# Attention scores in four row tiles, with q and k turned by VectorE

## The chip, the cores and the metric

One core of one Trainium2 chip. Times are device microseconds of that core, medians over several executions; "span" is the length of one profiled execution. The experiments ran as several jobs, on different chips, so each ratio is to the kernel before in the same job. TensorE, VectorE, ScalarE and GpSimd are called PE, DVE, ACT and POOL in the profile; PEld is the weight load of TensorE.

## The reference

Sliding-window attention with ALiBi (8 batches, 8 heads, 576 rows, head size 64, window 128), then a two-layer network with ELU on the 4608 resulting rows (512 to 2048 to 512):

```python
scores = scale * np.matmul(q, k.transpose(0, 1, 3, 2))
mask = (rel >= 0) & (rel < window)                       # rel = query position - key position
scores = np.where(mask, scores - slopes * np.abs(rel), -1e9)
attn = softmax(scores)
x = (attn @ v) ...reshape(B * S, H * D)
h = x @ w_in
out = np.where(h > 0, h, np.exp(np.minimum(h, 0)) - 1) @ w_out
```

One weakness of the comparison: the drawn q and k are small (0.1 times normal), so the scores hardly differ from the ALiBi term. "Right" below means right by construction.

## The kernel before

The kernel works in slots, emitted in order on every engine. A slot holds one piece of the hidden layer (`hp`, 8 or 16 matmuls), one quarter of an output block (`op`, 4 matmuls), and some attention work. In the kernel before, TensorE turns q and k with transposes into PSUM, and ScalarE and VectorE copy them out. ALiBi and mask enter as extra rows of the score matmul:

```python
def transposes(b, hp):                       # two heads a call
    t = ps_s.tile([128, 2, 2, 4, 2, 32], F16, name="tp", tag="sps")
    for g in range(2):
        for w in (1, 0):
            for j in range(2):
                nc.tensor.transpose(t[:, g, w, :, j, :], stq[b][...], ident)
    ...                                      # two copies to QK, by ACT or DVE

def mm(o, h, kc, qc, n):                     # scores: all 128 rows of the array
    nc.tensor.matmul(t[:, o:o + n], qk[0:r, h, 1, kc:kc + 128], qk[0:r, h, 0, qc:qc + n], ...)
e = ex[b, s] = EX[count[0] % 4]
nc.scalar.activation(e[:, 0:512], t, AF.Exp, scale=0.125)
# then cut(): DVE takes the minimum with a band

def hidden(t, j):
    ...                                      # hp <- xT, w_in
    nc.scalar.activation(e, p, AF.Exp)
    nc.gpsimd.tensor_scalar(out=e, in0=e, scalar1=1.0, scalar2=0.0, op0=ALU.min, op1=ALU.max)
def elu(t, j):                               # one slot later; frees one of the two hp banks
    V.scalar_tensor_tensor(out=gs[t][...], in0=e, scalar=1.0, in1=hp, op0=ALU.subtract, op1=ALU.max)
```

The q and k loads give partition p of each block of 128 rows the rows 4p to 4p+3, so the columns come out in another order, and masks, v and output rows are arranged to suit.

The softmax here doesn't subtract the row's maximum and nothing guards it: scores larger than these inputs give would overflow.

Of the kernel before, what the change touches and what calls it, by code (L numbers as in the profile page):

```python
# [10 lines left out]
I32 = mybir.dt.int32  # L11
# [4 lines left out]
BIG = 60000.0  # L16
# [3 lines left out]
def kernel(  # L20
# [13 lines left out]
    NP = H // 2  # L34
    NFC = FF // 128
    NTB = NTOK // 512
    MID = S // 2
    XBAR = 2
    RING = 3 * S
    VW = D + 2  # L40
    V = nc.vector
# [5 lines left out]
    ps_s = ctx.enter_context(tc.tile_pool(name="ps_s", bufs=2, space=PSUM))  # L47
    ps_v = ctx.enter_context(tc.tile_pool(name="ps_v", bufs=2, space=PSUM))
    ps_x = ctx.enter_context(tc.tile_pool(name="ps_x", bufs=1, space=PSUM))
# [7 lines left out]


    DM = one([128, 384], F16, "DM")
    cI = one([128, H, 128], F16, "cI")  # L60
    band = one([128, 384], F16, "band")




    QK = [one([128, H, 2, 640], F16, f"QK{i}") for i in range(2)]
    VP = [one([128, 5, H, VW], F16, f"VP{i}") for i in range(2)]
    EX = [one([128, 576], F16, f"EX{i}") for i in range(4)]
    w_in_sb = one([128, 4, FF], F16, "wi")
    w_out_sb = one([128, NFC, DO], F16, "wo")  # L70
    xT = one([128, 4, RING], F16, "xT")


    stq, stt, vf, vs = {}, {}, {}, {}

    def load_qk(b, w, h0=0, h1=H):

        if b not in stq:
            stq[b] = stage.tile([128, 2, H, 4, D], F16, name="stq")
        nc.gpsimd.dma_start(  # L80
            stq[b][:, w, h0:h1, :, :].rearrange("p h j d -> p h (j d)"),
            (q, k)[w][b, h0:h1, 0:512, :].rearrange("h (p j) d -> p h (j d)", j=4))

    def load_half(b, w, a):
        if b not in stq:
            stq[b] = stage.tile([128, 2, H, 4, D], F16, name="stq")
        nc.gpsimd.dma_start(
            stq[b][64 * a:64 * a + 64, w, :, :, :].rearrange("p h j d -> p h (j d)"),
            (q, k)[w][b, :, 256 * a:256 * a + 256, :].rearrange("h (p j) d -> p h (j d)", j=4))

    def load_v_half(b, a):
        if b not in vs:
            vs[b] = stage.tile([128, H, 4, D], F16, name="vs", tag="vs", bufs=2)
        nc.gpsimd.dma_start(
            vs[b][64 * a:64 * a + 64, :, :, :].rearrange("p h j d -> p h (j d)"),
            v[b, :, 256 * a:256 * a + 256, :].rearrange("h (p j) d -> p h (j d)", j=4))

    def load_tail(b, w):
        if b not in stt:
            stt[b] = stage.tile([64, 2, H, D], F16, name="stt")  # L100
        nc.gpsimd.dma_start(
            stt[b][:, w, :, :], (q, k)[w][b, :, 512:576, :].rearrange("h s d -> s h d"))

    def load_v4(b):

        vs[b] = stage.tile([128, H, 4, D], F16, name="vs", tag="vs", bufs=2)
        nc.gpsimd.dma_start(vs[b].rearrange("p h j d -> p h (j d)"),
                            v[b, :, 0:512, :].rearrange("h (p j) d -> p h (j d)", j=4))

    def load_v4_tail(b):  # L110
        nc.gpsimd.dma_start(VP[b % 2][0:64, 4, :, 0:D],
                            v[b, :, 512:576, :].rearrange("h s d -> s h d"))

    def place_v4(b, n):
        for j in range(4):
            V.tensor_copy(VP[b % 2][32 * j:32 * j + 32, n, :, 0:D],  # L116
                          vs[b][32 * n:32 * n + 32, :, j, :])

    def load_v(b, n):

        t = vf[b, n] = stage.tile([128, H, D], F32, name="vf", tag="vf", bufs=3)
        if b == 3 and n < 3:
            nc.gpsimd.memset(t[:, 0, 0:1], 0.0)
        if n < 4:
            for j in range(4):
                nc.sync.dma_start(
                    t[32 * j:32 * j + 32, :, :],
                    v[b, :, 128 * n + j:128 * n + 128:4, :].rearrange("h p d -> p h d"))
        else:
            nc.sync.dma_start(t[0:64, :, :], v[b, :, 512:576, :].rearrange("h p d -> p h d"))  # L130
# [11 lines left out]
    def load_wo(i, n):  # L142
        nc.gpsimd.dma_start(
            w_out_sb[:, 4 * i:4 * i + 4 * n, :],
            moe_w_out[512 * i:512 * i + 512 * n, :].rearrange("(c p) d -> p c d", p=128))
# [3 lines left out]
    with tc.manual_schedule():  # L149

        row = one([128, 1], I32, "row")
        col = one([128, 128], I32, "col")
        posi = one([128, 576], I32, "posi")
        nc.gpsimd.iota(row, pattern=[[0, 1]], base=0, channel_multiplier=1)
        nc.gpsimd.iota(col, pattern=[[1, 128]], base=0, channel_multiplier=0)
        load_half(0, 1, 0)
        load_half(0, 0, 0)
        nc.gpsimd.iota(posi[:, 0:512].rearrange("p (n j i) -> p n j i", j=4, i=32),
                       pattern=[[128, 4], [1, 4], [4, 32]], base=0, channel_multiplier=0)
        nc.gpsimd.iota(posi[:, 512:576], pattern=[[1, 64]], base=512, channel_multiplier=0)  # L160
        load_v_half(0, 0)
        load_wi(0)
        load_wi(1)
        load_half(0, 1, 1)
        load_half(0, 0, 1)
        load_v_half(0, 1)
        load_wi(2)
        load_wi(3)

        def small(name, dt=F32):  # L170
            return one([128, 1], dt, name)

        rowf = small("rowf")
        V.tensor_copy(rowf, row)
        V.tensor_scalar(out=ident, in0=col, scalar1=rowf, scalar2=None, op0=ALU.is_equal)
        for h in range(H):
            nc.scalar.mul(cI[:, h, :], ident, 8.0 * 2.0 ** (-8.0 * (h + 1) / H))

        kdiv, kmod, kpos = small("kdiv", I32), small("kmod", I32), small("kpos")
        V.tensor_scalar(out=kdiv, in0=row, scalar1=5, scalar2=None, op0=ALU.logical_shift_right)  # L180
        V.tensor_scalar(out=kmod, in0=row, scalar1=31, scalar2=None, op0=ALU.bitwise_and)
        V.scalar_tensor_tensor(out=kpos, in0=kmod, scalar=4.0, in1=kdiv, op0=ALU.mult, op1=ALU.add)
        for i in range(2):
            V.memset(VP[i][:, :, :, D:D + 1], 1.0)
        nd = one([128, 384], F32, "nd")
        nm = one([128, 384], F32, "nm")

        def seen(c, t, key, off, n):

            V.tensor_scalar(out=nd[:, c:c + n], in0=t, scalar1=key, scalar2=-1.0,  # L190
                            op0=ALU.subtract, op1=ALU.mult)
            if off:
                V.tensor_scalar(out=nd[:, c:c + n], in0=nd[:, c:c + n], scalar1=float(-off),
                                scalar2=None, op0=ALU.add)

        def unseen(c, n, bound, op):
            V.tensor_scalar(out=nm[:, c:c + n], in0=nd[:, c:c + n], scalar1=bound, scalar2=-BIG,
                            op0=op, op1=ALU.mult)

        def join(c, n):  # L200
            V.tensor_tensor(out=DM[:, c:c + n], in0=nd[:, c:c + n], in1=nm[:, c:c + n], op=ALU.add)

        seen(0, posi[:, 0:256], kpos, 0, 256)
        unseen(0, 128, 0.0, ALU.is_gt)
        unseen(128, 128, -127.0, ALU.is_lt)
        join(0, 256)

        def last_blocks():
            seen(256, posi[:, 512:576], kpos, -384, 64)
            seen(320, posi[:, 512:576], rowf, -512, 64)  # L210
            unseen(256, 64, -127.0, ALU.is_lt)
            unseen(320, 64, 0.0, ALU.is_gt)
            join(256, 128)

        def bands():
            V.tensor_scalar(out=band, in0=DM, scalar1=-1000.0, scalar2=BIG, op0=ALU.is_gt, op1=ALU.mult)

        def zeros():
            for i in range(2):
                V.memset(QK[i][0:64 + 64 * i, :, 1, 576:640], 0.0)  # L220
                V.memset(VP[i][64:128, 4, :, 0:D], 0.0)
            for e in EX:
                V.memset(e[:, 512:576], 0.0)


        g_, r_ = slice(64, 96), slice(96, 128)
        gof = small("gof")
        is96, is97, isx = small("is96"), small("is97"), small("isx")
        TQ = one([128, 576], F16, "TQ")
        TK = one([128, 640], F16, "TK")  # L230
        gi = one([128, 320], I32, "gi")
        pm = one([128, 576], F32, "pm")

        def groups():
            V.tensor_scalar(out=gof, in0=rowf, scalar1=-8.0, scalar2=1024.0, op0=ALU.mult, op1=ALU.add)
            V.tensor_scalar(out=gi[g_, 0:256], in0=posi[g_, 0:256], scalar1=gof[g_, :], scalar2=None,
                            op0=ALU.add)
            V.tensor_scalar(out=gi[g_, 256:320], in0=posi[g_, 512:576], scalar1=gof[g_, :],
                            scalar2=None, op0=ALU.add)
            V.tensor_scalar(out=gi[g_, :], in0=gi[g_, :], scalar1=255, scalar2=None,  # L240
                            op0=ALU.bitwise_and)

        def terms():

            V.tensor_scalar(out=is96, in0=rowf, scalar1=96.0, scalar2=None, op0=ALU.is_equal)
# [10 lines left out]
        def group_rows():  # L256
# [5 lines left out]
            for t in (TQ, TK):  # L262
                V.tensor_copy(t[g_, 256:512], t[g_, 0:256])
# [6 lines left out]
        def fill_k(i):  # L270
            nc.sync.dma_start(QK[i][r_, :, 1, :], QK[1 - i][r_, :, 1, :])

# [355 lines left out]
```

## Time and profile before

| | before |
|---|---|
| time, median | 366.84 us (366.28 to 369.29) |
| TensorE busy | 94% |
| VectorE busy | 67% |
| ScalarE / GpSimd busy | 57% / 40% |
| mean granted TensorE clock | 0.995 |

How to read it: TensorE is busy nearly throughout, and its work sets the end. The prediction shows the lines. One batch from the middle (busy us of each engine in the stretch, instruction counts in brackets, then clock and transfers):

```profile
195.78:232.55 36.77, 36.30 (x377) 26.70 (x377) 25.96 (x59) 23.58 (x40) 16.65 (x26) 1.00 0.67 111
```

In order: PE, PEld, DVE, ACT, POOL. TensorE has 36.3 of 36.8 us; VectorE has 11 us to spare.

### The profile page before, as it was taken

What the parts mean: (1) busy time and instruction counts of PE and PEld (TensorE: products, weight loads), DVE (VectorE), ACT (ScalarE), POOL (GpSimd) and SP (SyncE); (2) the same over time, 40 slices, a digit from 0 to 9 for tenths busy, and PEclk for the clock granted to TensorE, in tenths of its full rate; (3) what the DMA queues carried; (4) which work ended last, traced back from release to release, by engine and by line L of the source; (5) the groups of instructions that cost most, each with busy time, mean ns of one, the idle gap of its engine ahead of it and who ended that gap; (6) DMA issues with size and microseconds to landing.
All of it is one profiled execution on the core that took longest, in us unless ns stands there. A gap on an engine that the chain in (4) does not pass through costs nothing.

```text
span 363.7 us, 9613 instructions
## 1 busy us (share of the span) xinstructions
PE 340.3 (94%) x3790; PEld 251.6 (69%) x3790; DVE 243.5 (67%) x574; ACT 206.7 (57%) x349; POOL 145.7 (40%) x229
## 2 busy tenths in 40 slices
PE   6878997999979999989999999999999999999994
PEld 6766775777647667767777777777777777666651
DVE  6479889678886776666676767776776756634430
ACT  4355583666537655765566665666567565543431
POOL 9146623434314723472346334642433232233320
PEclk9899999999999999999999999999999999999999
DMA  8999999839243973497448934793631222211113
GB/s 114 198 206 119 228 107 183 151 80 155 38 103 89 133 108 84 110 128 110 98 94 127 127 88 100 120 136 82 102 84 45 52 47 45 51 43 47 29 43 73
DMA packets 81948, 37.06 MB, mean 102 GB/s; under 512 B 51952, under 2 KB 77296, under 8 KB 81904
## 3 DMA queue, kind: packets, MB, share of 16 engines
q0 software_dynamic: 34064, 15.40, 35.5%
q1 hardware_dynamic: 47840, 21.06, 25.6%
q8 instruction: 29, 0.48, 0.6%
q14 instruction: 15, 0.12, 0.1%
HBM read 36.70 MB, written 9.44 MB: 127 GB/s over the span
## 4 chain that ended last, share of the span: by engine, by line
PE 65%; DVE 14%; ACT 9%; DMA 7%; issue 3%; POOL 1%; SPq 0%; ACTq 0%; POOLq 0%
PE hp L451 27%; PE op L492 25%; PE sp L348 5%; ACT QK L322 5%; DVE VP L116 4%; DMA vs<-in_v_dram 3%; PE av L394 3%; DVE g L463 3%; ACT EX L372 2%; DVE QK L324 2%; ACT e L455 2%; DVE EX L380 2%; DMA xT<-xn 2%; DMA stq<-in_q_dram 1%; DVE xn L415 1%
## 5 line engine op out<-in xcount | busy, mean ns | idle before, releaser
L456 POOL TENSOR_SCALAR e<-e 128x512 f32<-128x512 f32 x144 | 88.6, 615 | 199.9 <-ACT e L455 199.9
L451 PE MATMUL hp<-xT,wi 128*128 128x256 f16 (+3 forms) x1536 | 150.3, 246 | 8.1 <-DVE g L463 3.6
L451 PEld LDWEIGHTS <-wi 128*128 128x128 f16 x1536 | 121.5, 98 | 49.9 <-DVE g L463 5.5
L455 ACT ACTIVATE e<-hp 128x512 f32<-128x512 f32 x144 | 86.0, 597 | 119.0 <-PE hp L451 110.0
L492 PE MATMUL op<-wo,g 128*128 128x512 f16 x576 | 146.4, 379 | 0.0
L463 DVE SCALAR_TENSOR_TENSOR g<-e,hp 128x512 f16<-128x512 f32 x144 | 98.0, 681 | 23.9 <-POOL e L456 22.7
L380 DVE TENSOR_TENSOR EX<-EX,band 128x512 f16<-128x512 f16 x112 | 49.8, 445 | 57.1 <-ACT EX L372 57.0
L372 ACT ACTIVATE EX<-sp 128x512 f16<-128x512 f32 x128 | 75.9, 593 | 13.3 <-PE sp L368 8.6
L492 PEld LDWEIGHTS <-g 128*128 128x128 f16 x576 | 51.2, 98 | 36.9
L348 PE MATMUL sp<-QK 128*128 128x128 f16 (+3 forms) x576 | 49.8, 213 | 0.0
L394 PE MATMUL av<-VP,EX 128*128 128x65 f16 x576 | 38.6, 193 | 4.3 <-DVE EX L380 2.7
L394 PEld LDWEIGHTS <-EX 128*128 128x128 f16 x576 | 31.6, 98 | 8.7 <-DVE EX L380 4.2
L415 DVE TENSOR_TENSOR xn<-av,rden 128x256 f16<-128x256 f32 x80 | 34.0, 424 | 2.8
L348 PEld LDWEIGHTS <-QK 128*128 128x128 f16 (+1 forms) x576 | 31.3, 97 | 1.0 <-issue 0.2
L496 ACT COPY ob<-op 128x512 f32<-128x512 f32 x36 | 21.1, 586 | 14.3 <-PE op L492 6.4
L322 ACT COPY QK<-tp 64x1024 f16<-64x1024 f16 x28 | 28.1, 1005 | 1.6 <-PE tp L312 1.4
L414 DVE RECIPROCAL rden<-av 128x4 f32<-128x4 f32 x80 | 14.4, 180 | 16.0 <-PE av L394 14.6
L134 POOL TENSOR_SCALAR VP<-vf 128x512 f16<-128x512 f32 (+1 forms) x25 | 19.5, 779 | 2.7 <-DMA vf<-in_v_dram 2.7
L324 DVE COPY QK<-tp 64x1024 f16<-64x1024 f16 x28 | 19.2, 684 | 1.1 <-PE tp L312 0.8
L312 PE MATMUL tp<-ident,stq 128*128 128x128 f16 x224 | 17.1, 219 | 2.3 <-ACT QK L322 1.0
L312 PEld LDWEIGHTS <-stq 128*128 128x128 f16 x224 | 13.8, 98 | 3.4 <-issue 3.2
L116 DVE COPY VP<-vs 32x512 f16<-32x512 f16 x48 | 14.9, 310 | 1.3 <-DMA vs<-in_v_dram 0.5
(70 smaller groups left out, 118.5 us busy)
## 6 DMA issues: line engine op xcount, KB each, us to landing
out_dram<-ob SPq DMA_DIRECT2D x128, 64.0 KB, 1.7
vf<-in_v_dram SPq DMA_DIRECT2D x80, 64.0 KB, 2.3
stq<-in_k_dram POOLq DMA_DIRECT2D x7, 512.0 KB, 6.4
stq<-in_q_dram POOLq DMA_DIRECT2D x7, 512.0 KB, 7.5
wi<-in_moe_w_in_dram POOLq DMA_DIRECT2D x4, 512.0 KB, 13.8
wo<-in_moe_w_out_dram POOLq DMA_DIRECT2D x4, 512.0 KB, 15.1
QK<-TQ SPq DMA_DIRECT2D x2, 576.0 KB, 8.0
vs<-in_v_dram POOLq DMA_DIRECT2D x2, 512.0 KB, 9.9
```

What stands on the lines that cost most here:

```text
L312: nc.tensor.transpose(t[:, g, w, :, j, :], stq[b][:, w, 2 * hp + g, 2 * j:2 * j + 2, :].rearrange("p a d -> p (a d)"), ident)
L322: nc.scalar.copy(o, i)
L348: nc.tensor.matmul(t[:, o:o + n], qk[0:r, h, 1, kc:kc + 128], qk[0:r, h, 0, qc:qc + n], start=b > 0 or o == 0, stop=b > 0)
L372: nc.scalar.activation(e[:, 0:512], t, AF.Exp, scale=0.125)
L380: V.tensor_tensor(out=e, in0=e, in1=band[:, c:c + n].unsqueeze(1).broadcast_to([128, 512 // n, n]), op=ALU.min)
L394: nc.tensor.matmul(a[:, l, :], e[:, c:c + 128], vp[:, n, h, 0:D + 1], start=st, stop=sp)
L415: V.tensor_tensor(out=xnt[b, i][:, 4 * half:4 * half + 4, :], in0=a[:, :, 0:D], in1=r.unsqueeze(2).broadcast_to([128, 4, D]), op=ALU.mult)
L451: nc.tensor.matmul(p[:, l * w + u0:l * w + u1], w_in_sb[:, c, fc * 128:(fc + 1) * 128], xT[:, c, x0:x0 + u1 - u0], start=(c == 0), stop=(c ...
L455: nc.scalar.activation(e, p, AF.Exp)
L456: nc.gpsimd.tensor_scalar(out=e, in0=e, scalar1=1.0, scalar2=0.0, op0=ALU.min, op1=ALU.max)
L463: V.scalar_tensor_tensor(out=gs[t][:, f0:f0 + nf, c0:c0 + w], in0=sh(es.pop((t, j))), scalar=1.0, in1=sh(hps.pop((t, j))), op0=ALU.subtrac ...
L492: nc.tensor.matmul(ops[t], gs[t][:, fc, ts * 128:(ts + 1) * 128], w_out_sb[:, fc, :], start=(fc == 0), stop=(fc == NFC - 1))
```

## The change

Its intent: run the scores with a contraction of 32 in four row tiles of TensorE, so that four heads go through the array at once; have VectorE turn q and k in squares of 32 (no TensorE transposes, no PSUM, no copies out); keep rows in natural order, so that one transfer loads large contiguous pieces and output rows go out in one; and put ALiBi and mask into a table that multiplies the exponentials. The core of the diff, cuts marked:

```diff
-    QK = [one([128, H, 2, 640], F16, f"QK{i}") for i in range(2)]
+    TAB = one([128, 2, 4, 512], F16, "TAB")
+    QT = [one([128, 2, 2, S], F16, f"QT{i}") for i in range(2)]
+    KT = [one([128, 2, 2, 640], F16, f"KT{i}") for i in range(2)]
+    sp = ps_s.tile([128, 4, 512], F32, name="sp", tag="sp")      # four banks, one set
...
+    def load_qk(b, w, g):                                        # R = 18
+        nc.gpsimd.dma_start(
+            st[b][32 * g:32 * g + 32, w, :, :, :].rearrange("p h r d -> p h (r d)"),
+            (q, k)[w][b, 2 * g:2 * g + 2, :, :].rearrange("h (i r) d -> i h (r d)", r=R))
+
+    def turn_qk(b, w, h2, dh):
+        o = (QT, KT)[w][b % 2][:, h2, dh, 0:S].rearrange("p (i r) -> p r i", r=R)
+        V.transpose(o, st[b][:, w, h2, :, 32 * dh:32 * dh + 32])
...
+    def scores(b, k_):
+        for o, kb, q0, n in parts:
+            for dh in range(2):
+                for g in range(4):
+                    r = slice(32 * g, 32 * g + 32)
+                    nc.tensor.matmul(sp[:, g, o:o + n], kt[r, h2, dh, ...], qt[r, h2, dh, ...],
+                                     start=dh == 0, stop=dh == 1, tile_position=(32 * g, 0))
...
+    def weigh(b, k_, gp):                                        # 1024 elements a call
+        V.tensor_tensor(out=e, in0=e, in1=t, op=ALU.mult)
...
+            order = [(w, h2, dh) for h2 in range(2) for w in (1, 0) for dh in range(2)]
+            for n, what in enumerate(order):
+                at(a - 4 + n, turn_qk, b, *what)                 # eight adjoining slots
```

Partition i holds the rows 18i to 18i+17. The transpose emits, for each r, 32 values for the rows 18i + r, so in natural order consecutive values lie 18 elements, 36 bytes, apart.

## The prediction

> **What bounds the kernel now.** I read the page's totals first, then the tail, where no attention is left, then the chain of waits, then the first 40 us. Totals and slices:
>
> ```profile
> PE 340.3 (94%) x3790; PEld 251.6 (69%) x3790; DVE 243.5 (67%) x574; ACT 206.7 (57%) x349; POOL 145.7 (40%) x229
> PE   6878997999979999989999999999999999999994
> PEclk9899999999999999999999999999999999999999
> ```
>
> TensorE sets the pace at full clock; only the first fifth has holes. The loop runs in slots: one piece of the hidden layer (hp), one quarter of an output block (op), and attention between. In the timeline's tail the slot is bare:
>
> ```profile
> 338.93 1.04 PE L451 MATMUL hp<-xT,wi 128*128 128x256 f16 x8
> 339.17 0.59 ACT L496 COPY ob<-op 128x512 f32<-128x512 f32 x1 [0.31 <-PE op L492]
> 339.80 1.03 PE L492 MATMUL op<-wo,g 128*128 128x512 f16 x4
> 340.00 0.60 ACT L455 ACTIVATE e<-hp 128x512 f32<-128x512 f32 x1 [0.24 <-PE hp L451]
> 340.66 1.04 PE L451 MATMUL hp<-xT,wi 128*128 128x256 f16 x8
> ```
>
> The starts 338.93, 339.80, 340.66 say 0.87 us for each half: 1.74 us a slot, and that cannot be moved by this change. In the chain of waits two like slots, one batch (16 slots) apart:
>
> ```profile
> 195.78 1.03 PE hp L451 x8
> ...
> 232.55 1.03 PE hp L451 x8
> ```
>
> 36.77 us a batch; less 16 x 1.74 = 27.8 leaves 9.0 us a batch for attention. Slots with attention but no transposes start every 2.08 us in the timeline, so scores and values take 16 x 0.34 = 5.5, and turning q and k the other 3.5. That 9.0 is what the change can attack.
>
> The start is different. The first hp begins at 16.7 us, and the next 15 take until 59 us, 2.8 us each: waits on transfers and on VectorE. One wait matters:
>
> ```profile
> 9.32 0.80 POOL L143 DMA_DIRECT2D wo<-in_moe_w_out_dram  x1
> 12.49 0.74 POOL L143 DMA_DIRECT2D wo<-in_moe_w_out_dram  x1 [2.36 <-DMA wi<-in_moe_w_in_dram]
> ```
>
> These are the 11th and 12th transfers of GpSimd's queue. The 12th shares no data with wi; it waited for the 4th issued. So a ninth transfer apparently can't be issued until the one eight before it has landed. Costs I reuse:
>
> ```profile
> L463 DVE SCALAR_TENSOR_TENSOR g<-e,hp 128x512 f16<-128x512 f32 x144 | 98.0, 681 | 23.9 <-POOL e L456 22.7
> L380 DVE TENSOR_TENSOR EX<-EX,band 128x512 f16<-128x512 f16 x112 | 49.8, 445 | 57.1 <-ACT EX L372 57.0
> L415 DVE TENSOR_TENSOR xn<-av,rden 128x256 f16<-128x256 f32 x80 | 34.0, 424 | 2.8
> L414 DVE RECIPROCAL rden<-av 128x4 f32<-128x4 f32 x80 | 14.4, 180 | 16.0 <-PE av L394 14.6
> L322 ACT COPY QK<-tp 64x1024 f16<-64x1024 f16 x28 | 28.1, 1005 | 1.6 <-PE tp L312 1.4
> L134 POOL TENSOR_SCALAR VP<-vf 128x512 f16<-128x512 f32 (+1 forms) x25 | 19.5, 779 | 2.7 <-DMA vf<-in_v_dram 2.7
> ```
>
> [...]
>
> **The change part by part.**
> TensorE, per batch. Gone: 32 transposes, the tail's, and the waits around them, 3.5 us. Scores: four calls, each streaming two half-depths of 512 columns in four tiles. The value matmuls before start 4 in 0.13 us, 32 ns for a pair of weight load and matmul; I take that as the floor. A call has 16 or 24 pairs, 0.51 or 0.77 us; two of each is 2.6 us. [...] Values: 72 x 32 ns = 2.3. Sum 5.7 against 9.0, 3.3 less.
>
> VectorE. From the two rows on PSUM, (681 - 424)/256 = 1.0 ns an element plus 167 ns. A transpose of 576 is then an estimated 0.75 us, eight a batch = 6.0. The weighing by the table, 1024 f16 at half that rate, 0.70, eight = 5.6. Elu 16 x 0.68 = 10.9, ten normalizings at 0.60 = 6.0. Sum 28.5 us in a batch that TensorE would do in 33.5: 85%, up from 71 to 73%. The transposes fall in eight adjoining slots, where VectorE has 17.9 us against TensorE's 16.7.
>
> ScalarE loses the 1.0 us copies (4 a batch); its exponentials stay 128.
>
> The start. Before any transpose, all 576 rows of q and k are needed, not half. GpSimd issues 20 transfers (8 q/k, 4 wi, 8 of the next batch) before the first cast of v. The last shares its place with the twelfth, wi's last. It lands when q, k, v and wi are through: 1.18 + 1.18 + 2.1 = 4.46 MB as counted at the destination, at the 200 GB/s of the early slices 22 us, from 3 us on: 25 us (before, hp waited for wi until 25.6). Then cast 0.8, and five us of values, normalizing, transposes and copies in series before hp: 31 us instead of 16.7. This is a guess from one observed wait.
>
> The count from there. Slots 0 to 12 have no output matmuls and are paced by VectorE; summing its work by the schedule gives 25 us, say 26. Slots 13 to 15 at 2.15, slots 16 to 19 (hp pauses) 6.5 in all: slot 20 at 70 us. From there 128 hp and 137 op at 0.87 = 230.6; 6.25 batches x 5.7 = 35.6: 336.
>
> Waits. Scores now go into one set of four banks, single-buffered: a call needs the last exponential of the call before, issued at the head of the same slot. Where ScalarE has an ob copy in front (0.31 + 0.59, then 0.60 of exponential and some 0.05) TensorE arrives after one hp, 0.87, and stands 0.65 us. By the schedule (ob after slots divisible by 4; scores in slots 1 mod 4 for batches 1, 2, 3, 5, 7) about 14 times: 9. VectorE's crowded slots 1 us a batch: 6. They partly coincide: 13. Sum 349.
>
> The end. Output now has one bank throughout: two waits of 0.95 for its copy, then copy and one transfer instead of four: 5.4. Span 354.6; the measured time exceeds the span by 3.1 (366.84 - 363.7): about 358. Both waiting terms are on the high side, so I say 356.
>
> **Rivals.**
> 1. The start is not held up and row tiles run near the ideal: hp from 23 us, attention 4.5 a batch, stalls half: about 338 us. For it: only one wait shows the limit of eight, and the TensorE saving is sure in sign. Against: the profile named a DMA as releaser, with no data in common.
> 2. VectorE becomes the bound. If strided writes make a transpose 1.3 us, a batch has 33 us of VectorE and the crowded slots run 4 us over each: about 372. For: the writes step 36 bytes. [...]
> 3. The tiles don't overlap [...]: attention is 9.9, no gain, and the late start remains: about 380. [...]
> 4. The saving is real but exactly given back by the start and the wait of scores for the exponentials: 361 to 366, "the same". Quite possible; the sums differ by only some us.
>
> **Range and chances.** The sum's main uncertain terms are the start (-8, +4), attention (-7, +9) and waits (-8, +10), independent: some 10 us either way. Range 342 to 368. Faster by 2% means under 359.5: 0.58. Within 2%: 0.36. Slower (over 374), only by rivals 2 or 3: 0.06.
>
> **What would show it.** Right: no copy from tp left; scores in calls of 0.5 to 0.8 us between hp and op; VectorE transposes near 0.75 us and weighings near 0.70; first hp near 31 us with the cast of v held by a transfer on GpSimd's queue; holes of about 0.65 us before scores, ended by ScalarE, where an ob copy precedes; 16-slot batches at 34 to 37 us. Wrong: a first hp near 23 us, or transposes over 1 us with elu as the releaser of hp, or score calls over 1.2 us.

Passages that rest on no trace of the kernel before are cut and marked. One was a term of the sum: the 5.7 us of attention a batch are 2.6 + 2.3 and 0.8 us that are cut. Over 6.25 batches that is 5.0 us of the 336, and so of the 349, the 354.6 and the 356 predicted; the 33.5 us of TensorE a batch and rival 3's 9.9 hold the same 0.8. How far row tiles overlap (24 pairs in 0.77 us, rival 1's 4.5 us a batch, rival 3's 9.9), and that a transpose takes 1.0 ns an element, were estimates: the kernel before has neither tiles nor transposes on VectorE. The "half that rate" of the weighing agrees with the row L380: 445 ns less 167, over 512 elements, is 0.54 ns each.

## The result, and the profile after

The changed kernel took 462.74 us (461.14 to 464.51), before 366.56 us in the same rounds. The ratio is 1.2604 (95% interval 1.2545 to 1.2663): 26% slower, far outside the range.

From the page of the changed kernel: totals, the slices for TensorE and its clock, and the chain that ended last, by engine:

```profile
PE 338.5 (73%) x3280; PEld 226.8 (49%) x3280; DVE 346.7 (75%) x453; ACT 176.9 (38%) x317; POOL 155.6 (34%) x265
PE   4017467756697669987699468966698569999996
PEclk9555765979799797988889999999999897999999
DVE 44%; PE 37%; DMA 9%; issue 5%; ACT 3%; POOL 2%; DVEq 0%; ACTq 0%; POOLq 0%
```

VectorE has more to do than TensorE, and the chain runs through it more than through TensorE. TensorE now has holes to the end of the attention, and its mean granted clock is 0.88 (before, 0.995). The groups (line, engine, operation, shapes, count, then busy us and mean ns of one):

```profile
L76 DVE STREAM_TRANSPOSE KT<-st 128x576 f16<-128x576 f16 x32 | 84.4, 2660 | 10.5 <-DMA st<-in_k_dram 10.3
L76 DVE STREAM_TRANSPOSE QT<-st 128x576 f16<-128x576 f16 x32 | 84.3, 2655 | 0.0
L171 DVE TENSOR_TENSOR EX<-EX,TAB 128x1024 f16<-128x1024 f16 x64 | 48.1, 754 | 1.1 <-ACT EX L160 0.9
```

A transpose takes 2.66 us, where the prediction had 0.75; the weighing, 0.75, is near the 0.70 predicted. The waits name the consequence (engine and line, what it waited for: total us, times, longest):

```profile
PE hp L222 <- DVE g L234: 57.7, 36, 2.6
PE sp L154 <- DVE QT L76: 43.4, 17, 13.5
```

The first of them in the timeline of one crowded slot (start us, us, engine and line):

```profile
267.11 2.65 DVE L76 STREAM_TRANSPOSE KT<-st 128x576 f16<-128x576 f16 x1
269.25 0.61 POOL L227 TENSOR_SCALAR e<-e 128x512 f32<-128x512 f32 x1 [3.23 <-ACT e L226]
269.40 0.88 DVE L234 SCALAR_TENSOR_TENSOR g<-e,hp 128x512 f16<-128x512 f32 x1
270.33 1.03 PE L222 MATMUL hp<-xT,wi 128*128 128x256 f16 x8 [0.69 <-DVE g L234]
270.74 2.63 DVE L76 STREAM_TRANSPOSE KT<-st 128x576 f16<-128x576 f16 x1
273.94 0.27 PE L222 MATMUL hp<-xT,wi 128*128 128x256 f16 x1 [1.72 <-DVE g L234]
```

In this trace VectorE runs its instructions in the program's order: elu (start 273.02 us) comes after the transpose issued before it (270.74, 2.63 us), elu frees the hp bank, and the next hp waits 1.72 us for it. hp starts 3.6 us apart here; with short transposes (the contiguous version below) it is 2.1 on average, 37.4 us for 18. A batch, from one hp to the like one 18 slots on:

```profile
270.33:321.31 50.98, 37.55 (x369) 24.86 (x369) 42.96 (x55) 21.28 (x39) 18.09 (x32) 1.00 0.42 80
```

TensorE's own work is small, as predicted: 37.6 us for 18 slots, where before had 36.3 for 16. But VectorE has 43.0, and the batch takes 51.0. The clock in this stretch is 1.00: the loss is not the clock's here.

### The profile page after: what moved, and what is told of

It reads as the page before. It is cut to its first block, busy times and chain, and to the rows that moved or that the text cites. A ratio compares the mean times of both kernels' runs of the same rounds, so it can differ in the third digit from the quotient of the medians.

```text
span 462.2 us, 8158 instructions
## 1 busy us (share of the span) xinstructions
PE 338.5 (73%) x3280; PEld 226.8 (49%) x3280; DVE 346.7 (75%) x453; ACT 176.9 (38%) x317; POOL 155.6 (34%) x265
## 4 chain that ended last, share of the span: by engine, by line
DVE 44%; PE 37%; DMA 9%; issue 5%; ACT 3%; POOL 2%; DVEq 0%; ACTq 0%; POOLq 0%
PE op L243 18%; DVE QT L76 17%; PE hp L222 15%; DVE KT L76 14%; DMA st<-in_k_dram 7%; DVE g L234 6%; DVE EX L171 3%; DVE xn L189 3%; PE sp L154 3%; PE av L183 2%; DMA st<-in_q_dram 2%; ACT EX L160 1%; DVE rden L188 1%; ACT e L226 1%; POOL e L227 1%
## 5 line engine op out<-in xcount | busy, mean ns | idle before, releaser
L222 PE MATMUL hp<-xT,wi 128*128 128x256 f16 (+3 forms) x1408 | 163.7, 269 | 57.7 <-DVE g L234 57.7
L243 PE MATMUL op<-wo,g 128*128 128x512 f16 x576 | 157.3, 400 | 1.4 <-ACT ob L247 1.4
L234 DVE SCALAR_TENSOR_TENSOR g<-e,hp 128x512 f16<-128x512 f32 x144 | 108.5, 753 | 53.0 <-POOL e L227 53.0
L76 DVE STREAM_TRANSPOSE KT<-st 128x576 f16<-128x576 f16 x32 | 84.4, 2660 | 10.5 <-DMA st<-in_k_dram 10.3
L76 DVE STREAM_TRANSPOSE QT<-st 128x576 f16<-128x576 f16 x32 | 84.3, 2655 | 0.0
L154 PE MATMUL sp<-QT,KT 32*128 32x256 f16 (+2 forms) x640 | 27.0, 284 | 48.1 <-DVE QT L76 43.4
L171 DVE TENSOR_TENSOR EX<-EX,TAB 128x1024 f16<-128x1024 f16 x64 | 48.1, 754 | 1.1 <-ACT EX L160 0.9
L154 PEld LDWEIGHTS <-KT 32*128 32x128 f16 x640 | 15.6, 99 | 57.7 <-issue 40.4
L183 PE MATMUL av<-VP,EX 128*128 128x65 f16 x576 | 33.7, 202 | 9.8 <-DVE xn L189 8.0
L70 POOL DMA_DIRECT2D st<-in_k_dram x32 | 18.3, 571 | 5.8 <-DMA wi<-in_moe_w_in_dram 5.1
L70 POOL DMA_DIRECT2D st<-in_q_dram x32 | 18.0, 563 | 5.3 <-DMA wi<-in_moe_w_in_dram 4.8
```

Source lines behind the costliest of these rows:

```text
L70: nc.gpsimd.dma_start(st[b][32 * g:32 * g + 32, w, :, :, :].rearrange("p h r d -> p h (r d)"), (q, k)[w][b, 2 * g:2 * g + 2, :, :].rearran ...
L76: V.transpose(o, st[b][:, w, h2, :, 32 * dh:32 * dh + 32])
L154: nc.tensor.matmul(sp[:, g, o:o + n], kt[r, h2, dh, 128 * kb:128 * kb + 128], qt[r, h2, dh, q0:q0 + n], start=dh == 0, stop=dh == 1, tile_ ...
L171: V.tensor_tensor(out=e, in0=e, in1=t, op=ALU.mult)
L183: nc.tensor.matmul(a[:, g, :], e[:, g, c:c + 128], VP[b % 2][:, n, 2 * g + h2, 0:D + 1], start=j == 0, stop=j == len(parts) - 1)
L222: nc.tensor.matmul(p[:, l * w + u0:l * w + u1], w_in_sb[:, c, fc * 128:(fc + 1) * 128], xT[:, c, x0:x0 + u1 - u0], start=(c == 0), stop=(c ...
```

## The experiments

Twelve kernels ran. The theory: the transposes' duration is the whole loss, through VectorE's load, and the output step of 36 bytes is what makes them slow. The rivals: a transpose of 2-byte elements is slow by itself; the load on the engine, or GpSimd working at the same time, makes it slow; or the loss is partly elsewhere (clock, waits for ScalarE, crowding).

### Forms of the transpose

The changed kernel with twelve forms on scratch tiles appended where VectorE is otherwise idle; the output is unaffected.

```diff
+        for _ in range(3):
+            V.transpose(step(18), rows)     # L375: as in the kernel, 36 bytes
+        for _ in range(3):
+            V.transpose(cont, rows)         # L377: output contiguous, input as in the kernel
+        ...                                 # L379 step 18, input contiguous; L381 both contiguous;
+                                            # L383 step 20; L385 step 32; L387 every second element;
+                                            # L389 plain copy, step 18; L391 plain copy, contiguous;
+                                            # L393 4-byte elements, step 18; L395 4-byte, contiguous
```

> The changed kernel, with twelve forms of VectorE instruction on scratch tiles behind it, three of each, at a time when VectorE has nothing else to do. In the changed kernel a transpose of 576 f16 took 2.66 us, 4.3 ns an element after some 170 ns, where the prediction had 1.0. Theory A (the output's step of 36 bytes): the transposes into a contiguous output take 0.7 to 0.8 us and those with the step 2.6, and a plain copy into the step is slow as well. Theory B (a transpose of 2-byte elements is slow by itself): all f16 transposes take about 2.6 us, contiguous or not, and a 4-byte one of as many elements takes about 0.75. Theory C (the load on the engine [...]made it slow): all forms are at 0.75 us here, where GpSimd is idle.

The groups of the appended lines:

```profile
L375 DVE STREAM_TRANSPOSE dst<-src 128x576 f16<-128x576 f16 x3 | 7.9, 2645 | 0.1
L377 DVE STREAM_TRANSPOSE dst<-src 128x576 f16<-128x576 f16 x3 | 2.3, 778 | 0.1
L379 DVE STREAM_TRANSPOSE dst<-src 128x576 f16<-128x576 f16 x3 | 7.9, 2639 | 0.1
L389 DVE COPY dst<-src 128x576 f16<-128x576 f16 x3 | 4.2, 1399 | 0.1
L391 DVE COPY dst<-src 128x576 f16<-128x576 f16 x3 | 0.9, 310 | 0.1
```

L375 to L377 differ in the output step alone: 2.65 against 0.78 us. The input pattern is nothing (L379), the engine's load is nothing (idle here, still 2.65), and the transpose as such is nothing (contiguous: 0.78, close to the 0.75 predicted). A plain copy is slower too, 1.40 against 0.31, though not all of that is the 36 bytes: with a step of 6 bytes it takes 0.65 (second set, below). Steps of 40 and 64 bytes took 2.70 and 2.68, every second element (4 bytes) 0.82; 4-byte elements 1.26 with a step of 72 bytes and 0.78 contiguous. So a transpose of 2-byte elements is not slow by itself, and neither the load nor GpSimd (idle here) makes it so: both rivals on the transpose fall as they were put. The width does count once there is a step, though (2.65 against 1.26). This was one execution, timed by its profile only.

How the cost grows with the step, from a second set:

```diff
+        for _ in range(3):
+            V.transpose(step(dst, 2), by(flat, 2))    # L374; then steps 3, 6, 9: L376, L378, L380
+        ...                                           # 4-byte elements, steps 2, 3, 6, 9: L382 to L388
```

> Again forms of VectorE instruction behind the changed kernel, now with small output steps: transposes of 576 f16 with steps of 2, 3, 6 and 9 elements (4, 6, 12, 18 bytes), of 576 4-byte elements with steps of 2, 3, 6 and 9 (8, 12, 24, 36 bytes), and plain copies. The first set gave 0.78 us contiguous, 0.82 at 4 bytes (stepping over every second element), and 2.64 to 2.70 at 36, 40 and 64 bytes; 4-byte elements 0.78 contiguous and 1.26 at 72 bytes. Theory A1 (the cost grows with the step[...]): 6, 12, 18 bytes lie between, near 0.9, 1.3 and 1.8. Theory A2 (any step [...]costs the full 2.6): 6 bytes and up all 2.6, and the 4-byte elements flat at about 1.26 from 8 bytes on.

```profile
L374 DVE STREAM_TRANSPOSE dst<-src 128x576 f16<-128x576 f16 x3 | 2.5, 823 | 0.1
L376 DVE STREAM_TRANSPOSE dst<-src 128x576 f16<-128x576 f16 x3 | 3.4, 1143 | 0.1
L378 DVE STREAM_TRANSPOSE dst<-src 128x576 f16<-128x576 f16 x3 | 6.3, 2092 | 0.1
L380 DVE STREAM_TRANSPOSE dst<-src 128x576 f16<-128x576 f16 x3 | 8.1, 2691 | 0.1
L382 DVE STREAM_TRANSPOSE dst<-src 128x576 f32<-128x576 f32 x3 | 2.3, 780 | 0.1
```

Both sets together, for one transpose of 576 elements:

| output step, bytes | 2 | 4 | 6 | 8 | 12 | 18 | 24 | 36 | 64 | 72 |
|---|---|---|---|---|---|---|---|---|---|---|
| f16, us | 0.78 | 0.82 | 1.14 | | 2.09 | 2.69 | | 2.65 | 2.68 | |
| 4-byte, us | | 0.78 | | 0.78 | 0.94 | | 1.19 | 1.20 | | 1.26 |

Theory A1, growth with the step, is right in kind, though its 0.9, 1.3 and 1.8 us were too low; A2 falls at 6 and 12 bytes (1.14 and 2.09 us). The growth for f16 stops between 12 and 18 bytes (2.09 and 2.69; 2.65 at 36). The 4-byte elements lose nothing at 8 bytes (0.78 us) and take 0.94 at 12. Three more rows of the second set (4-byte transpose, step 36 bytes; f16 copy, 6; 4-byte copy, 36) show that the step in bytes is not the whole of it:

```profile
L388 DVE STREAM_TRANSPOSE dst<-src 128x576 f32<-128x576 f32 x3 | 3.6, 1203 | 0.1
L392 DVE COPY dst<-src 128x576 f16<-128x576 f16 x3 | 2.0, 652 | 0.1
L396 DVE COPY dst<-src 128x576 f32<-128x576 f32 x3 | 2.0, 680 | 0.1
```

At 36 bytes the f16 transpose takes 2.65 us and the 4-byte one 1.20, the f16 copy 1.40 and the 4-byte one 0.68. And the f16 copy at 6 bytes loses nothing against 4 bytes (0.65 and 0.79), where the transpose does (1.14 and 0.82). So the width of the element and the kind of instruction count as well. That the output step makes the transpose slow is shown; why it does is not.

### The same instructions with a contiguous output

```diff
-        o = (QT, KT)[w][b % 2][:, h2, dh, 0:S].rearrange("p (i r) -> p r i", r=R)
+        o = (QT, KT)[w][b % 2][:, h2, dh, 0:S].rearrange("p (r i) -> p r i", i=32)
```

The result is wrong (columns in another order); every count stays.

> The changed kernel with the transposes' output contiguous, so that the columns of q and k are in another order and the result is wrong on purpose; as many instructions and elements as before. If the output step is the cause, a transpose takes about 0.75 us, VectorE's load falls by 64 x 1.9 = 122 us, and the time lands near the 356 us predicted (345 to 370). If a 2-byte transpose is slow by itself, nothing changes: 455 to 465 us.

355.07 us (352.94 to 356.73), ratio to before 0.9666 (0.9606 to 0.9726). One output pattern is worth some 108 us (by medians of two jobs; the ratios say the same), and the time comes out at the 356 predicted, though partly by luck, as told below. Its profile: the transposes, and the batch that answers to those shown above (18 slots):

```profile
L76 DVE STREAM_TRANSPOSE KT<-st 128x576 f16<-128x576 f16 x32 | 24.4, 767 | 10.3 <-DMA st<-in_k_dram 10.3
...
165.30:202.70 37.40, 36.54 (x370) 24.81 (x369) 28.09 (x55) 21.51 (x39) 20.12 (x32) 1.00 0.59 116
```

VectorE has 28.1 instead of 43.0 us, TensorE is the bound again, and the batch takes 37.4 instead of 51.0. From 110 us to 320 us the granted clock is 1.00, where the changed kernel had 0.92 in the same stretch. Nothing but the transposes' output was touched, so the lower clock came with the slow transposes. Holes in TensorE's work as such do not explain it: in the spread version below TensorE was busy 169 of these 210 us at a clock of 0.99, in the changed kernel 162 at 0.92. How much of the 108 us the clock passed on was not tried alone.

### No transposes after the first batch

```diff
-            qt, kt = QT[b % 2], KT[b % 2]
+            qt, kt = QT[0], KT[0]
...
-                at(a - 4 + n, turn_qk, b, *what)
+                pass
```

> The changed kernel without the transposes of batches 1 to 7 (they use batch 0's q and k; the result is wrong on purpose). The first batch still has its eight long transposes at the start. If the transposes are the whole of the loss, and the other steps of the prediction hold, the time is the predicted 356, plus some 9 us of later start, less 10 to 15 us of the 0.75 us transposes and their crowding: 345 to 360 us. If the slower TensorE clock of 0.88, or the waits of the scores for ScalarE, carry a good part by themselves, it stays above 390.

352.92 us (352.58 to 353.92), ratio 0.9608 (0.9568 to 0.9647). Its output is wrong, which doesn't matter for the time. The 2 us to the contiguous version are within the intervals, and they are not what short transposes cost: batch 0's eight stay long here, and hp begins at 39.8 us instead of 33.7. From there to the end it takes 311.3 us, in the contiguous version 320.2. So seven batches of transposes at 0.77 us, with their waits for loads, cost up to some 9 us; most of their 43 us hide beside TensorE. The clock and the waits for ScalarE carry nothing of this size by themselves.

### Load or crowding

The slow transposes kept, but spread: for batches 2 to 7 one in every second slot.

```diff
-                at(a - 4 + n, turn_qk, b, *what)
+                at(a - 12 + 2 * n if b > 1 else a - 4 + n, turn_qk, b, *what)
```
(and the loads eight slots earlier)

> The changed kernel with its slow transposes kept, but for batches 2 to 7 one in every second slot instead of one in each of eight adjoining slots (the loads eight slots earlier). It tells VectorE's total load from its crowding. VectorE's work is some 28.5 + 8 x 1.9 = 43.8 us in 16 slots, above TensorE's 33.5, so if the total is what counts a batch of 18 slots falls from the 51 us measured only to 45 or 46, and the time to 425 to 440 us. If crowding were the whole loss, it would fall to 365 to 390. If neither, it stays at 460.

427.73 us (424.24 to 428.19), ratio 1.165 (1.1605 to 1.1695). Some 35 us went with the crowding (adjoining slots, more work in each than a slot lasts); the clock rose too, from 0.88 to 0.92 in the mean, and the two were not separated. A batch of 18 slots fell from 51.0 to 47.4 us (from hp at 236.38 us to 283.73), where 45 or 46 was expected. The larger part stays, as VectorE's work per batch, 42.5 us in this stretch, is above TensorE's 38.6.

### Pairs of f16 as one 4-byte element

Half as many transposes, each still of 576 elements, in every second slot; the scores read every second element. Right by construction, since q and k are split into the same even and odd halves.

```diff
+    def turn_qk(b, w, h2):
+        o = (QT, KT)[w][b % 2][:, h2, 0:S, :].rearrange("p s d -> p (s d)").bitcast(F32)
+        i = st[b][:, w, h2, :, :].rearrange("p r d -> p (r d)").bitcast(F32)
+        V.transpose(o.rearrange("p (i r) -> p r i", r=R), i.rearrange("p (r d) -> p r d", d=32))
...
-                             sp[:, g, o:o + n], kt[r, h2, dh, 128 * kb:128 * kb + 128],
+                             sp[:, g, o:o + n], kt[r, h2, 128 * kb:128 * kb + 128, dh],
```

> The changed kernel with pairs of f16 transposed as one 4-byte element: four transposes a batch instead of eight, 576 elements each, written with a step of 72 bytes; the scores read every second element; the result is right. Theory A (the output step): a transpose stays near 2.6 us or gets slower, but there are half as many: VectorE loses 32 x 2.66 = 85 us, and the time is 375 to 400 us. Theory B (2-byte elements): each takes about 0.75 us and the time is 340 to 360 us. Rival on TensorE: operands with a step of 4 bytes slow the scores, calls of over 1 us instead of 0.5.

360.11 us (359.53 to 361.26), ratio 0.981 (0.9771 to 0.985): faster, though whether by 2% is unclear. Neither expectation was right on the duration: 1.25 us, between them, as the forms showed. The operands' step of 4 bytes costs the scores nothing: 21.6 us busy over all score matmuls, as in the contiguous version. Why this version stays 5 us above the contiguous one, with less VectorE work in transposes (40 against 49 us), is open.

### Rows in pairs: natural order with a small step

If a partition holds pairs of neighbouring rows (64m + 2i + j), the transposed values lie 4 bytes apart and the columns stay natural. The price is loads in pieces of 512 bytes instead of 4608.

```diff
-            (q, k)[w][b, 2 * g:2 * g + 2, :, :].rearrange("h (i r) d -> i h (r d)", r=R))
+            (q, k)[w][b, 2 * g:2 * g + 2, :, :].rearrange("h (m i j) d -> i h m (j d)", i=32, j=J))      # J = 2
...
-        o = (QT, KT)[w][b % 2][:, h2, dh, 0:S].rearrange("p (i r) -> p r i", r=R)
+        o = (QT, KT)[w][b % 2][:, h2, dh, 0:S].rearrange("p (m i j) -> p m j i", i=32, j=J)
...
```

> A right version of the changed kernel: the load gives each partition pairs of neighbouring rows (64m + 2i + j instead of 18i + r), so the transposes write with a step of 4 bytes and the columns stay in natural order; the q and k loads fall apart into pieces of 512 bytes instead of 4608. If the output step is the whole of it, transposes take 0.82 us and the time is that of the contiguous version plus 64 x 0.04: 354 to 360 us. If the smaller pieces slow the loads, the first hidden layer starts later than 33.7 us and the time is up to 365.

353.51 us (352.44 to 354.1), ratio 0.9628 (0.9595 to 0.9661), right, and just under what was expected. Transposes 0.81 us; the first hp at 34.9 us against 33.7, but that of slot 20 at 76.9 against 77.0: the smaller pieces cost next to nothing. With the 4-byte pairs as well (a step of 8 bytes):

> The same rows, and pairs of f16 transposed as 4-byte elements with a step of 8 bytes: four transposes a batch. If those take 0.8 us, VectorE has 3.3 us a batch less than with pairs of rows alone. As TensorE is the bound in most slots of the contiguous version, that is worth little: 350 to 357 us. If the crowded VectorE slots still mattered, 340 to 348.

352.04 us (350.8 to 352.87), ratio 0.9589 (0.9556 to 0.9622), right; transposes 0.77 us, four a batch. Halving them gives almost nothing, as VectorE is no longer the bound.

### The start and the copy of the output

Three more edits try two other terms of the prediction on the version just told. First the start: batch 1's eight loads issued after the casts of v.

> The version before with one more edit: the eight loads of batch 1's q and k are issued after the casts of batch 0's v, not before. My prediction said that the casts stood behind a transfer held until wi's last had landed. If so, the casts begin about 10 us earlier (near 15 us instead of 26), the first hidden layer begins at 22 to 25 us instead of 33.7, and the time falls by 5 to 10 us. Rival: the time is set by when wi lands (hp needs all of it in its first four slots) or by VectorE's work in slots 1 to 8, and the gain is under 3 us.

351.46 us (349.79 to 351.68), ratio 0.9566 (0.9535 to 0.9598): within the interval of the version without it. The first hp does begin 7.9 us earlier, at 27.4 instead of 35.3, but the fourth piece stands still (I had counted it as the third):

```profile
38.17 0.78 DVE L78 STREAM_TRANSPOSE KT<-st 128x576 f32<-128x576 f32 x1 [6.00 <-DMA st<-in_k_dram]
38.88 0.65 DVE L237 SCALAR_TENSOR_TENSOR g<-e,hp 128x512 f16<-128x512 f32 x1
...
39.58 1.23 PE L225 MATMUL hp<-xT,wi 128*128 128x128 f16 x10 [5.92 <-DVE g L237]
```

VectorE stands 6.0 us at batch 1's first transpose, whose data now comes late, with an elu behind it in the queue. One wait was exchanged for another.

Next, the copy of a finished output block is put behind the exponentials at the head of the next slot (on top of the edit before):

```diff
+                late.append((t, ts))
...
             for f, a in early.get(s, []):
                 f(*a)
+            store()                     # the copy to ob and its transfer
```

> The last right version (rows in pairs, 4-byte transposes, batch 1's loads after the casts), with the copy of a finished output block moved behind the exponentials at the head of the next slot. The prediction put 14 waits of 0.65 us on this copy standing before the exponential that the scores wait for; the profile of that version shows 14 waits of scores for ScalarE, 7.6 us. If they are on the path: those waits go to under 2 us and the time falls by 4 to 7 us, from 351.5 to 345 to 348. If they were only taking up time that VectorE's lag takes anyway: under 2 us.

346.94 us (345.94 to 349.98), ratio 0.9457 (0.9404 to 0.9511). The waits of the scores for ScalarE, 14 of 7.6 us in the version before it, became:

```profile
PE sp L157 <- ACT EX L163: 2.8, 2, 2.2
```

As expected, these waits were on the path: the time fell by 4.5 us by the medians, 4.0 by the ratios (two jobs), and the two intervals do not meet. With wi as one transfer and batch 1's last load in slot 0 as well:

> The same, with wi loaded as one transfer instead of four, and batch 1's last load in slot 0: GpSimd's queue then has one transfer to wait for instead of four. In the version before, hp stood 9.3 us after its second piece while GpSimd waited for wi's transfers to land. If that hold-up is the start's limit, hp's third piece begins near 32 us instead of 39.6 and the time falls by 3 to 7 us against the run without this edit. If the arrival of wi itself is, the first pieces of hp only shift, and the gain is under 2 us.

347.16 us (344.85 to 347.66), ratio 0.9437 (0.9393 to 0.9482): no gain. hp's fourth piece came at 39.0 us, again behind VectorE's wait for batch 1's k (3.75 us). So the last kernel takes that place in the queue: the late-copy version with batch 1's transposes in slots 3, 4, 6 and 7.

```diff
-                at(a - 4 + 2 * n, turn_qk, b, *what)
+                at(a - 4 + 2 * n if b > 1 else (a - 2, a - 1, a + 1, a + 2)[n], turn_qk, b, *what)
```

> The late-copy version with one more edit: batch 1's four transposes in slots 3, 4, 6 and 7 instead of 1, 3, 5 and 7. In the two versions before, VectorE stood 6.0 and 3.75 us at the first of them, waiting for batch 1's k, with elu of earlier hidden pieces behind it in its queue, and hp waited for that elu. If this place in the queue is the start's limit, hp's third piece begins near 34 us instead of 40.7, and the time falls by 3 to 6 us, from 347 to 341 to 344. If the late arrival of k just moves the same wait to batch 1's scores, or TensorE's first slots are bound otherwise, under 1.5 us.

344.08 us (342.79 to 346.55), ratio 0.9351 (0.9303 to 0.9399), against 0.9457 for the version without it (another job, so each against its own runs of before). hp's fourth piece begins at 34.3 us instead of 40.7. The gain (2.9 us by the medians, 3.9 by the ratios) is at the low end of what was expected, and part of the wait only moved: two pieces later hp stands 2.0 us behind the same transpose. This version is right and beats both kernels: 6.5% faster than before.

## Why the prediction was wrong

**The step that failed is the size of one term.** "A transpose of 576 is then an estimated 0.75 us, eight a batch = 6.0": measured 2.66, eight a batch = 21.3. The difference, 64 x 1.9 = 122 us of VectorE, makes VectorE the bound, and the time is 108 us above that of the same kernel with short transposes. The estimate came from instructions with contiguous output, and the prediction saw the step and waved it off in rival 2, with an argument that no trace showed. That rival had the cause, with half the duration (1.3 us) and a small chance. The trace of before shows no transpose on VectorE, and none was measured before predicting.

**The other steps**, read in the version with the contiguous output and the right ones after it:

- The whole sum: 356 predicted, 355.07 with the transposes at 0.77 us. Two errors cancel in it. The start is later than predicted (hp's first piece at 33.7 us, not 31; that of slot 20 at 77.0, not 70), and from there to the end it took 276.9 us, where 354.6 - 70 = 284.6 was predicted. Most of these 7.7 us are the waits: 13 us were put, and from slot 20 on TensorE waited 3.7 us for exponentials and 2.3 for elu.
- Attention: 5.7 us a batch, and waits of 13 us over all, were predicted. A batch of 18 slots takes 37.4 us; less 18 x 1.74 = 31.3, 6.1 us are left with the waits in it.
- The row tiles: 24 pairs were put at 0.77 us. In the contiguous version's timeline a call starts at 171.93 us and the next matmul at 172.48: 0.55 us for 4,096 columns (four tiles of 1,024), where hp's 2,048 take 0.87. That is 3.2 times the rate. hp starts 0.97 us before the call; less its 0.87, some 0.10 us pass; what they go to is not shown. Rival 3 falls.

```profile
170.96 1.03 PE L222 MATMUL hp<-xT,wi 128*128 128x256 f16 x8
171.93 0.62 PE L154 MATMUL sp<-QT,KT 32*128 32x256 f16 x24
172.48 1.04 PE L243 MATMUL op<-wo,g 128*128 128x512 f16 x4
```

- The start: the casts of v behind a transfer held for wi's last, at about 25 us: in the changed kernel they begin at 26.1. The guess from one wait was right: the 17th to 20th transfers of GpSimd's queue waited 9.9 us in all for wi's four, the 9th to 12th. Whether the chip or the program's semaphores set this limit is not shown. That this holds up the whole start was half right: moving the loads alone gained nothing, since VectorE's queue held the next wait.
- The waits of scores for the exponential behind an ob copy: 14 of 0.65 us, 9 us. Measured in the contiguous version: 14 waits of 7.4 us, and taking most of them away gave 4.0 to 4.5 us. The number of waits and the path were right, the size was not, and the sum fits by luck: three of the 14, 3.7 us, belong to the start, and the other eleven last 0.34 us on average (3.7 in all), not 0.65.
- Crowded slots: 6 us were predicted with short transposes. From slot 20 on the contiguous version has 2.3 us of hp waiting for elu. The mechanism is what the changed kernel shows at full size.
- The prediction left TensorE at full clock; it fell to 0.88, with the slow transposes. What sets it stays open.
- One reading was loose: the 1.0 ns an element is the difference of two rows of different instructions, 681 ns for 512 elements of a scalar_tensor_tensor and 424 for 256 of a tensor_tensor.

## What to carry to other kernels

Cost an instruction by its output pattern as well as by its element count: on VectorE, transposes of f16 that stored 18 bytes or more apart took over three times as long as with a contiguous output (2.64 to 2.70 us against 0.78). Where a layout forces a step, choose the load so that neighbouring rows share a partition; pairs (a step of 4 bytes, 0.81 us) were enough here, and cost the loads next to nothing (first hp at 34.9 us against 33.7). And ask of every wait that is taken away what stands next in the same queue (here an elu behind VectorE's 6.0 us wait for batch 1's k).
